# RWKV-6 attention and an exact-GELU MLP on one core: a new order for the first tile, its second tile's loads apart from the weight pieces, and odd chunks of one unit's y in the other partition half

## The chip, the cores and the metric

The kernel runs on one core of one Trainium2 chip. The metric is device time in microseconds (us); lower is better. TensorE is called PE (its weight loads PEld), VectorE DVE, ScalarE ACT, GpSimd POOL, and the queue of SyncE, which issues nearly all transfers, SP.

## The reference

Four sequences of 768 tokens with 8 heads of 48 go through a gated linear recurrence. Its result, as 3072 rows of 384, goes through two matrix products with an exact GELU between them. r, k, v, w, u are float32; the two weight matrices come as float64.

```python
for t in range(S):
    cur = einsum('bhd,bhe->bhde', u[None] * kt, vt)
    y[:, :, t] = einsum('bhd,bhde->bhe', rt, state + cur)
    state = wt[:, :, :, None] * state + einsum('bhd,bhe->bhde', kt, vt)
x = y.transpose(0, 2, 1, 3).reshape(3072, 384)
h = x @ w_in                                   # 384 x 2048
out = (0.5 * h * (1 + erf(h / sqrt(2)))) @ w_out   # 2048 x 384
```

## The kernel before, in words

**Tiles.** There are 8 tiles (NX) of 384 tokens. A tile holds four pairs of heads; the two heads of a pair lie in partitions 0 to 63 and 64 to 127, and the tokens are cut into chunks of 64, six to a tile, even and odd ones taken as pairs. attention(x, unit) computes one tile's y: products of k and r by levels (L485, for tile 1 also L501, for later tiles L653), whose masked parts go to a_sb (DVE L581, ACT L578), decay products on DVE (L552, L563), k transposed on PE (kt_ps L754) and copied to SBUF by ACT (L767), k times v (kv_ps L804), the states chained on DVE (st L836, L831), and y from two sets of products into the same banks: a_sb times v (L857), then the state times r (L900), with small DVE reads (the fences, L867 and L870) between the sets. y is copied to xT, the transposed input of the MLP. Its rows of the fourth pair go through ysb (ACT L926) and three transfers each on SP and ACT (L930).

**The first tile** is the one tile cut into two units: unit 0 holds pairs 0 and 1, unit 1 holds pairs 2 and 3. Each unit has 24 small matmuls for each product. Unit 0's y lies in two single banks, one for even and one for odd chunks (the code calls this split); unit 1's lies in a pair of banks. The small matmuls use one quarter of the PE array each: 64 rows by 64 columns, where the rows are the operands' partition half and the columns are the partition half of the result. In L857 of unit 0 the row half is the chunk's parity p and the column half is the head g. In L900 the row half is the head g and the column half is g too.

**mlp(x)** multiplies a tile by w_in (h_ps L1290 for tiles 0 and 1, L1078 for later ones), applies GELU on ACT (L1293, L1295), and multiplies by w_out (o_ps L1384 for tile 0, L1304 for later ones). Tile 1 and later use sums of weight blocks (t, made on DVE at L946) to save products.

**Weights.** Each matrix comes in 8 pieces of 768 KB (16 in all). A float64 piece goes to a buffer raw (five of them), ACT makes two parts of each number (f L355; e L356 and L358), and DVE shifts and adds them (L367, L371) into w_in_sb or w_out_sb. The first three pieces come in three transfers of 256 KB each, and ahead of each transfer stands a 4-byte DVE write (L229) that holds the transfer back to that point of DVE's order. Tile 1's r, k, w come in eight shares of 288 KB, held back in the same way (L188).

**The order of the work** is written out by hand. Each piece of work is a generator; PLAN holds, for each round x, a string in which one letter takes one step of one stream. What a step issues goes into each engine's own queue in that order, and each queue runs in order. In round 0 the streams are: "." unit 0, "s" unit 1, "f" the beginning of tile 1's attention, "c" weight conversions, "w" the load of tile 1's v, "l" the transfers of the first three weight pieces with tile 1's shares put between them. In round 1 and later "." is mlp(x-1), "s" the rest of tile x's attention, "f" the beginning of the next tile's, "l" the loads of tile x+1, "c" (round 1) the conversions, "w" and "x" sums of weights and of x. After a string, what is left in the streams is issued stream by stream.

Of the kernel before, what the change touches and what calls it, by code (L numbers as in the profile page):

```python
# [21 lines left out]
C = 64  # L22
G = 64
D = 48
T = 384
Q = 2
# [10 lines left out]
NC_SP = 8  # L37
HALFWAY = 2
PLAN = {
    0: ".lls.....sslsc.lsslll.sl.sls.f.sl.lfscsl..sfss.lscfs.lscs.s.ssssclll..s...sss..cs...sw.ccff",  # L40
    1: (
        ".c.scccl..lscssc.cccscxcl..ccc.cscclcccc..ccscs.ccc.cc.ccss.cccccs.c.wcwccssss..c.ccss.ccl"
        ".sswwww.cccccccslwcclllf....sslc...cc...sf.fs.ffff...fffwffwwwwwlc"
    ),
    2: "....s...slw.sswssl.sssss...ss.sss.swsllsslwsww...s...sl..www.wslss..lcs.s.lf.sl..fx.w.xxx....sxxfff.....l",
    3: (
        "wscl..ss..s..sss....s...l.s.ssssssss..s..l.ss...sss..sllssss.ss...s...s...s...sllsssllf.sl"
        ".ff.fxxlx.xx....sffxfff"
    ),
    4: (  # L50
        "......llls..ss.....s....sss..ssss.....llssss..s...ssss...s..lssc..ss.....ssllsss..lfs..lfs"
        ".f..sffx..x.xffxxwfff.xl"
    ),
    5: ".......s...l.lls.s...s..ssssslssss...ss....sss.ssssss...s...ss...l.s..lslllfsss..c.sfffs..l..lwfxxx.xxx.",
    6: (
        "ss.ss....s...s....ss...s...sssls.slss....sss...s...ssss..lss...s..sscw....lll.ssll..sssslf"
        "..sf.f.ffll.x..x.x.ffsffxxx"
    ),
    7: (
        "......s..s...s.s...sss.ss.ss.sss..ss...wwwsss..swssswcs.ss.ww....l.s.wwwsww.wwww..ws.s.ss."  # L60
        "s.wwwwwswwwwww.ww.xxxxxww..xxx.wwsxx.x"
    ),
}

# [12 lines left out]
def kernel(  # L77
# [25 lines left out]
    nc = tc.nc  # L103
# [45 lines left out]
    half = [slice(0, 64), slice(64, 128)]  # L149
# [226 lines left out]
    def attention(x, unit):  # L376

        first = x % HALVES == 0
        parts = range(NPART) if units_of(x) == 1 else range(unit, unit + 1)
# [5 lines left out]
        r, k, w = (bufs[0 if x == 0 or i == 0 and x % 2 == 0 else 1][:, base + i * n_u:base + (i + 1) * n_u]  # L385
                   for i in range(3))
# [6 lines left out]
        xT = xT_of[x]  # L393
# [350 lines left out]
        if x < 2:  # L744
# [49 lines left out]
        def vs(b, i, g):  # L794
            o = ((parts[b] * NI + i) * 2 + g) * D
            return loaded[x][1][:, o:o + G]
# [39 lines left out]
                        nc.vector.tensor_copy(out=stq[:, b * Q:(b + 1) * Q, c], in_=kvs[b][:, :, 0, 0])  # L836


        def swap(b):
            return parts[b] % 2  # L840


        split = x == 0 and parts[0] == 0
        ys = []

        def inside():

            for b in range(np_):
                if split:
                    y = [ps.tile([128, BANK], F32, name="y_ps", tag="mm", bufs=2) for _ in range(2)]  # L850
                else:
                    y_ps = pair("y_ps")
                    y = [y_ps[:, c] for c in range(2)]
                for i in range(NI):
                    for p in range(2):
                        for g in range(2):
                            nc.tensor.matmul(y[p][half[g ^ swap(b)], i * C:(i + 1) * C], lhsT=vs(b, i, g)[half[p]],  # L857
                                             rhs=at[half[p], g, b * NI + i, :], start=(i == 0), stop=True, skip_group_check=True)
                ys.append((y, None if split else y_ps))

# [29 lines left out]
        for i in range(NI):  # L890
            for p in range(2):
                for b in range(np_):
                    q, c3 = divmod(i, N3)
                    for g in range(2):
                        c = 2 * c3 + (p + g) % 2
                        src, c0 = (st, c - 1) if c else (before, NC - 1)
                        if src is None:
                            continue
                        o = ((parts[b] * Q + q) * NC + c0) * D
                        nc.tensor.matmul(ys[b][0][c % 2][half[g ^ swap(b)], i * C:(i + 1) * C],  # L900
                                         lhsT=src[half[g], o:o + G], rhs=rc[half[g], b, i, c % 2],
                                         start=False, stop=True, skip_group_check=True)
        if split:
            for c, copy in enumerate((nc.scalar.copy, nc.vector.tensor_copy)):
                for z in range(2):
                    s = slice(z * G, z * G + D)
                    copy(out=xT[s, 0:Q, :].rearrange("p q (i c t) -> p (q i) c t", c=2, t=C)[:, :, c, :],
                         in_=ys[0][0][c][s, 0:NI * C].rearrange("p (i t) -> p i t", t=C))
            yield
            return  # L910
# [531 lines left out]
    def next_v():  # L1442
        load_v(1, nc.sync)
        yield
# [94 lines left out]
```

## Time and profile before

| what | value |
|---|---|
| median of 3 runs | 586.36 us (585.44 to 586.76) |
| the profiled execution's own time | 586.0 us |
| its span, first to last instruction | 584.1 us |
| PE busy over the span | 570.4 us (98%) |
| DVE, ACT, POOL busy | 460.1 (79%), 286.8 (49%), 8.1 us (1%) |
| granted PE clock | 1.0 |
| first h_ps matmul of tile 0 (L1290) | 44.3 us |
| first o_ps matmul of tile 1 (L1304) | 111.4 us |

In the page's view of 40 slices PE is at nine tenths or more from the fourth slice on; the first three slices, some 44 us, are tile 0's attention. The span from 44 to 111 us is round 1: tile 0's MLP with tile 1's attention. In a timeline row the first number is the start, the second the stretch, then come engine, line, operation and count; in square brackets is the idle time before it and what ended that. "issue" means that the engine waited for nothing that the profile shows. A float32 matmul is recorded as two, each with a weight load of its own.

### The profile page before, as it was taken

To read this page: it belongs to the slowest core of one execution; us is meant where nothing else is said; L and a number is where in the kernel's file an instruction comes from. 1 tells how busy PE (TensorE), PEld (TensorE's weight loads), DVE (VectorE), ACT (ScalarE), POOL (GpSimd) and SP (SyncE) were. 2 spreads that over 40 slices of the span, in tenths; PEclk is the share of its full clock that TensorE was granted. 3 is DMA by queue.
4 is the path that set the end of the run, shared out by engine and by line. 5 is a ranking of instruction groups with operands and counts; after the bars stand their busy time and mean duration, and the time that the engine had idled before them with its cause. 6 is when DMAs were issued, how large, how long until landed. Compare 5 with 4: busy or idle time off the path is not lost.

```text
span 584.1 us, 17192 instructions
## 1 busy us (share of the span) xinstructions
PE 570.4 (98%) x7418; PEld 505.7 (87%) x7418; DVE 460.1 (79%) x820; ACT 286.8 (49%) x672; POOL 8.1 (1%) x21
## 2 busy tenths in 40 slices
PE   7879999999999999999999999999999999999997
PEld 3566566756899999999999999999999999999997
DVE  6879769998879895888859988598859999965532
ACT  2576997332722567336553466345562367423400
POOL 3100000000000000000000000000000000000000
PEclk9999999999999999999999999999999999999999
DMA  7659741220232302341023201440014200210000
GB/s 240 205 158 372 255 171 57 77 80 2 36 103 75 111 2 39 95 122 57 1 55 120 76 21 22 111 140 2 3 34 146 72 3 2 43 39 7 1 15 34
DMA packets 51002, 46.78 MB, mean 80 GB/s; under 512 B 31728, under 2 KB 36080, under 8 KB 50928
## 3 DMA queue, kind: packets, MB, share of 16 engines
q1 hardware_dynamic: 50832, 45.62, 26.0%
q8 instruction: 58, 0.95, 0.7%
q14 instruction: 16, 0.13, 0.1%
q10 hardware_dynamic: 96, 0.07, 0.1%
HBM read 36.24 MB, written 4.72 MB: 70 GB/s over the span
## 4 chain that ended last, share of the span: by engine, by line
PE 93%; DMA 2%; ACT 2%; DVE 1%; issue 1%; SPq 0%; DVEq 0%; ACTq 0%
PE o_ps L1304 35%; PE h_ps L1078 16%; PE u_ps L1078 12%; PE h_ps L1290 11%; PE d L653 4%; PE o_ps L1384 4%; PE kv_ps L804 2%; PE y_ps L857 2%; PE y_ps L900 2%; PE c_ps L1078 2%; PE d L485 2%; DMA rkw<-in_rkw_dram 1%; DMA raw<-in_w_in_dram 1%; PE d L644 0%; ACT a_sb L669 0%
## 5 line engine op out<-in xcount | busy, mean ns | idle before, releaser
L1078 PE MATMUL h_ps<-xT,w_in_sb 128*128 128x192 f32 x408 | 81.5, 331 | 0.0
L1078 PEld LDWEIGHTS h_ps<-xT,w_in_sb 128*128 128x128 f32 x408 | 67.7, 190 | 3.0 <-ACT g L1110 1.1
L1290 PE MATMUL h_ps<-xT,w_in_sb 128*128 128x384 f32 x192 | 64.3, 491 | 0.0
L1290 PEld LDWEIGHTS h_ps<-xT,w_in_sb 128*128 128x128 f32 x192 | 35.7, 190 | 24.6 <-ACT rkw L1295 0.9
L1304 PE MATMUL o_ps<-w_out_sb,g 128*128 128x192 f32 x224 | 39.5, 326 | 0.0
L1304 PEld LDWEIGHTS o_ps<-w_out_sb,g 128*128 128x128 f32 x224 | 37.0, 190 | 0.3
L669 ACT COPY a_sb<-d 32x256 f32<-32x256 f32 (+8 forms) x90 | 32.6, 362 | 4.0 <-PE d L653 2.5
L1304 PE MATMUL o_ps<-w_out_sb,e 128*128 128x192 f32 x176 | 31.3, 329 | 0.0
L1304 PE MATMUL o_ps<-w_out_sb,f 128*128 128x192 f32 x176 | 31.1, 329 | 0.0
L1304 PE MATMUL o_ps<-t,e 128*128 128x192 f32 x176 | 30.9, 328 | 0.0
L1304 PE MATMUL o_ps<-t,s 128*128 128x192 f32 x176 | 30.9, 328 | 0.0
L1304 PE MATMUL o_ps<-t,g 128*128 128x192 f32 x176 | 30.8, 329 | 0.0
L1078 PE MATMUL u_ps<-s,w_in_sb 128*128 128x192 f32 x160 | 29.6, 328 | 0.0
L1304 PEld LDWEIGHTS o_ps<-t,g 128*128 128x128 f32 x176 | 28.7, 190 | 0.3
L1304 PEld LDWEIGHTS o_ps<-w_out_sb,e 128*128 128x128 f32 x176 | 28.7, 190 | 0.3
L1304 PEld LDWEIGHTS o_ps<-t,s 128*128 128x128 f32 x176 | 28.8, 190 | 0.2
L1304 PEld LDWEIGHTS o_ps<-t,e 128*128 128x128 f32 x176 | 28.8, 190 | 0.2
L1304 PEld LDWEIGHTS o_ps<-w_out_sb,f 128*128 128x128 f32 x176 | 28.7, 190 | 0.3
L1293 ACT ACTIVATE g<-h_ps 128x256 f32<-128x256 f32 (+1 forms) x32 | 13.8, 432 | 29.3 <-PE h_ps L1290 29.0
L485 PEld LDWEIGHTS d<-rkw 64*64 64x64 f32 x1056 | 17.3, 135 | 12.5 <-issue 6.9
L653 PE MATMUL d<-kx,rkw 64*64 64x96 f32 x1056 | 27.8, 247 | 0.2 <-ACT a_sb L669 0.2
L686 DVE COPY_PREDICATED a_sb<-quarter,d 128x480 f32<-128x480 uint8 (+5 forms) x54 | 23.1, 438 | 6.3 <-PE d L653 5.0
(247 smaller groups left out, 1188.2 us busy)
## 6 DMA issues: line engine op xcount, KB each, us to landing
rkw<-in_rkw_dram SPq DMA_DIRECT2D x54, 256.0 KB, 3.5
raw<-in_w_out_dram SPq DMA_DIRECT2D x8, 768.0 KB, 4.9
v_in<-in_v_dram SPq DMA_DIRECT2D x8, 584.0 KB, 4.3
raw<-in_w_in_dram SPq DMA_DIRECT2D x5, 768.0 KB, 6.6
out_dram<-o_sb SPq DMA_DIRECT2D x20, 192.0 KB, 2.0
rkw<-kx SPq DMA_DIRECT2D x72, 48.0 KB, 2.0
rkw<-in_rkw_dram SPq DMA_DIRECT2D x6, 384.0 KB, 6.8
raw<-in_w_in_dram SPq DMA_DIRECT2D x9, 256.0 KB, 4.2
```

The source lines that it names most:

```text
L485: nc.tensor.matmul(d[half[p], g, n * width:(n + 1) * width], lhsT=kc[half[g], b, i, p], rhs=right(half[g], b, i, p), start=True, stop=True)
L653: nc.tensor.matmul(o[half[p], i * 3 * C // 2:(i + 1) * 3 * C // 2], lhsT=kc[half[g], n // NI, n % NI, p], rhs=rx[half[g], 2 * n + p], star ...
L669: nc.scalar.copy(out=at[z, g, first:behind, (a + 1) * h:], in_=d[z, :, :, to] if g == slice(None) else d[z, :, to])
L686: nc.vector.copy_predicated(out=an[:, :, :, :, (a + 1) * h:], mask=mask.to_broadcast(data.shape), data=data)
L804: nc.tensor.matmul(kv_ps[half[g], p, i * D:(i + 1) * D], lhsT=k_t(b, i, p, g), rhs=vs(b, i, g)[half[p], 0:D], start=True, stop=True)
L857: nc.tensor.matmul(y[p][half[g ^ swap(b)], i * C:(i + 1) * C], lhsT=vs(b, i, g)[half[p]], rhs=at[half[p], g, b * NI + i, :], start=(i == 0 ...
L900: nc.tensor.matmul(ys[b][0][c % 2][half[g ^ swap(b)], i * C:(i + 1) * C], lhsT=src[half[g], o:o + G], rhs=rc[half[g], b, i, c % 2], start= ...
L1078: nc.tensor.matmul(o, lhsT=lhsT, rhs=rhs, start=start, stop=True, skip_group_check=True)
L1290: nc.tensor.matmul(h_ps, lhsT=w_in_sb[:, f // FI, j, f % FI * 128:(f % FI + 1) * 128], rhs=xT[:, j, :], start=(j == 0), stop=(j == NJ - 1))
L1293: nc.scalar.activation(out=gs[group][:, f % FG, 0:t], in_=h_ps[:, 0:t], func=AF.Gelu)
L1304: nc.tensor.matmul(o, lhsT=lhs(j), rhs=rhs(j), start=start and j == 0, stop=(j == HF - 1), skip_group_check=True)
L1384: nc.tensor.matmul(o, lhsT=block(i, f // HF, f % HF), rhs=w_out_sb[:, f, :], start=(f == 0), stop=(f == NF - 1))
```

## The change

Three things are changed.

1. PLAN's strings for rounds 0 and 1 are written anew. The strings for rounds 2 to 7 get two more turns of all streams at their ends.
2. Tile 1's eight shares, which stood between the weight pieces in stream "l", become a stream of their own, "x".
3. In unit 0 of tile 0, L900 and L857 put the odd chunks' y in the other partition half than the head (swap now returns the chunk's parity c instead of 0), and the copies to xT bring them back (to = z ^ c).

The instructions of the program are the same but for these partition halves and for a few of the wait instructions. On PE, ACT and SP the order differs in rounds 0 and 1 alone; on DVE the weight sums t (L946) come somewhat later and the order is the same again in round 2. The changed file has six more lines ahead of the kernel's code, so that L900 is its L906.

```diff
 PLAN = {
-    0: ".lls.....sslsc.lsslll.sl.sls.f.sl.lfscsl..sfss.lscfs.lscs.s.ssssclll..s...sss..cs...sw.ccff",
+    0: "...sls..l.sxsss.sflcl.sx.ls.l.l.lfsss..sxscxxxsss.x.s..cxss.lsfsssxxfs..s..cl..sscs...wwss.ccls..ffcw",
     1: (
-        ".c.scccl..lscssc.cccscxcl..ccc.cscclcccc..ccscs.ccc.cc.ccss.cccccs.c.wcwccssss..c.ccss.ccl"
-        ".sswwww.cccccccslwcclllf....sslc...cc...sf.fs.ffff...fffwffwwwwwlc"
+        "xc..ccss..cccssc.cccc..sssccc.cccccss.scccccsc.cc.ss.ssswccc.c.ssslcc..scllc...cc.lll.cs.c"
+        "cccclcccllsf.c.xfcccclfl.l.ccc.cc.cffccffff...c.wwsw..w.w...sw.fffxlwwwsswwwww"
     ),
...
-        def swap(b):
-            return parts[b] % 2
+        def swap(b, c):
+            return c if split else parts[b] % 2
...
-                            nc.tensor.matmul(y[p][half[g ^ swap(b)], i * C:(i + 1) * C], lhsT=vs(b, i, g)[half[p]],
+                            nc.tensor.matmul(y[p][half[g ^ swap(b, p)], i * C:(i + 1) * C], lhsT=vs(b, i, g)[half[p]],
...
-                        nc.tensor.matmul(ys[b][0][c % 2][half[g ^ swap(b)], i * C:(i + 1) * C],
+                        nc.tensor.matmul(ys[b][0][c % 2][half[g ^ swap(b, c % 2)], i * C:(i + 1) * C],
...
-                    s = slice(z * G, z * G + D)
-                    copy(out=xT[s, 0:Q, :].rearrange("p q (i c t) -> p (q i) c t", c=2, t=C)[:, :, c, :],
+                    s, to = (slice(a * G, a * G + D) for a in (z, z ^ c))
+                    copy(out=xT[to, 0:Q, :].rearrange("p q (i c t) -> p (q i) c t", c=2, t=C)[:, :, c, :],
...
-                ".": units[0], "s": units[1], "f": following, "c": pieces_of_w, "w": next_v(), "x": iter(()),
-                "l": chain(weight_in(0, True), islice(second, 5), weight_in(1, True), weight_in(2, True), second),
+                ".": units[0], "s": units[1], "f": following, "c": pieces_of_w, "w": next_v(), "x": second,
+                "l": chain(*(weight_in(i, True) for i in range(3))),
```

In queue terms: SP had two parts of the first weight piece, its third, five shares, the six parts of pieces two and three, piece four, then three shares. Now it has two parts, a share, the third part, a part of piece two, a share, two parts of piece two, two of piece three, six shares, the last part of piece three, piece four. In ACT's queue of round 0, where conversions of three pieces stood, two stand; the third comes after unit 0's copies to xT. The eight copies L578 now come ahead of the third of the four pairs L429, L431 (tile 1's scaled r). On PE the last product of unit 0 (24 matmuls of L485) now comes ahead of unit 1's kt_ps instead of behind it. DVE's first L371 moves from ahead of unit 0's last L552 to behind unit 1's state chain.

More of the change, by code (lines that the diff above doesn't have):

```diff
@@ L39 @@
 PLAN = {
-    0: ".lls.....sslsc.lsslll.sl.sls.f.sl.lfscsl..sfss.lscfs.lscs.s.ssssclll..s...sss..cs...sw.ccff",
+    0: "...sls..l.sxsss.sflcl.sx.ls.l.l.lfsss..sxscxxxsss.x.s..cxss.lsfsssxxfs..s..cl..sscs...wwss.ccls..ffcw",
     1: (
-        ".c.scccl..lscssc.cccscxcl..ccc.cscclcccc..ccscs.ccc.cc.ccss.cccccs.c.wcwccssss..c.ccss.ccl"
-        ".sswwww.cccccccslwcclllf....sslc...cc...sf.fs.ffff...fffwffwwwwwlc"
-    ),
-    2: "....s...slw.sswssl.sssss...ss.sss.swsllsslwsww...s...sl..www.wslss..lcs.s.lf.sl..fx.w.xxx....sxxfff.....l",
+        "xc..ccss..cccssc.cccc..sssccc.cccccss.scccccsc.cc.ss.ssswccc.c.ssslcc..scllc...cc.lll.cs.c"
+        "cccclcccllsf.c.xfcccclfl.l.ccc.cc.cffccffff...c.wwsw..w.w...sw.fffxlwwwsswwwww"
+    ),
+    2: (
+        "....s...slw.sswssl.sssss...ss.sss.swsllsslwsww...s...sl..www.wslss..lcs.s.lf.sl..fx.w.xxx."
+        "...sxxfff.....l.slxwc.slxwc"
+    ),
     3: (
         "wscl..ss..s..sss....s...l.s.ssssssss..s..l.ss...sss..sllssss.ss...s...s...s...sllsssllf.sl"
-        ".ff.fxxlx.xx....sffxfff"
+        ".ff.fxxlx.xx....sffxfff.slxwc.slxwc"
     ),
@@ L51 @@
         "......llls..ss.....s....sss..ssss.....llssss..s...ssss...s..lssc..ss.....ssllsss..lfs..lfs"
-        ".f..sffx..x.xffxxwfff.xl"
+        ".f..sffx..x.xffxxwfff.xl.slxwc.slxwc"
     ),
-    5: ".......s...l.lls.s...s..ssssslssss...ss....sss.ssssss...s...ss...l.s..lslllfsss..c.sfffs..l..lwfxxx.xxx.",
+    5: (
+        ".......s...l.lls.s...s..ssssslssss...ss....sss.ssssss...s...ss...l.s..lslllfsss..c.sfffs.."
+        "l..lwfxxx.xxx..slxwc.slxwc"
+    ),
     6: (
         "ss.ss....s...s....ss...s...sssls.slss....sss...s...ssss..lss...s..sscw....lll.ssll..sssslf"
-        "..sf.f.ffll.x..x.x.ffsffxxx"
+        "..sf.f.ffll.x..x.x.ffsffxxx.slxwc.slxwc"
     ),
@@ L60 @@
         "......s..s...s.s...sss.ss.ss.sss..ss...wwwsss..swssswcs.ss.ww....l.s.wwwsww.wwww..ws.s.ss."
-        "s.wwwwwswwwwww.ww.xxxxxww..xxx.wwsxx.x"
+        "s.wwwwwswwwwww.ww.xxxxxww..xxx.wwsxx.x.slxwc.slxwc"
     ),
```

## The prediction

> **What bounds the kernel now.** I read the share of each engine first, then the busy time by stage, then the chain that ended last, then ACT's and PE's timelines where that chain leaves PE. By stage (from, to, length, then busy time of PE, PEld, DVE, ACT, POOL, each with its count):
>
> ```profile
> 9.76:44.25 34.49, 27.89 (x1072) 21.33 (x1073) 28.46 (x76) 19.16 (x37) 2.89 (x5) 1.00 0.56 183
> 44.25:111.40 67.15, 67.15 (x943) 42.76 (x941) 56.54 (x81) 50.92 (x85) 0.00 (x0) 1.00 0.56 197
> ```
>
> The change reorders these two stages. In the second PE is never idle, and PE has the same matmuls there after the change, so a new order can gain next to nothing there and can only lose. In the first PE is idle for 6.6 us. The chain shows who holds it (start, us, what):
>
> ```profile
> 21.80 4.33 DMA raw<-in_w_in_dram
> 26.23 0.93 ACT f L355
> 27.16 0.92 ACT e L356
> ...
> 33.70 0.95 PE kv_ps L804 x48
> 34.65 0.81 PE kt_ps L754 x6
> 35.45 0.86 PE y_ps L857 x48
> 36.99 1.24 issue
> 38.89 1.84 DVE st L831 x10
> 40.91 1.32 PE y_ps L900 x36
> 42.34 1.98 PE d L501 x94
> ```
>
> Tile 0's y waits for kv_ps, and kv_ps for ACT, which is late because a weight piece landed late. ACT's timeline of that stretch:
>
> ```profile
> 26.23 0.93 ACT L355 ACTIVATE f<-raw 128x768 f32<-128x768 f32 x1 [3.95 <-DMA raw<-in_w_in_dram]
> 27.07 1.01 ACT L356 ACTIVATE e<-raw,two 128x768 f32<-128x768 uint32 x1
> 28.10 1.08 ACT L358 ACTIVATE e<-raw 128x768 f16<-128x768 f32 x1
> 30.58 2.57 ACT L578 COPY a_sb<-d 16x192 f32<-16x192 f32 x8
> 33.17 0.86 ACT L767 COPY g<-kt_ps 128x384 f32<-128x384 f32 x2
> 35.16 0.86 ACT L767 COPY g<-kt_ps 128x384 f32<-128x384 f32 x2 [0.30 <-PE kt_ps L754]
> ```
>
> ACT stood 3.95 us for the second piece, converted it, scaled two pairs of r (29.05 to 30.67) and then made the eight copies L578, so that kt_ps, done at about 31.7, was copied only from 33.17. The second thing that holds PE is the line "issue". PE's timeline between two such gaps:
>
> ```profile
> 19.50 0.45 PE L485 MATMUL d<-rkw 64*64 64x64 f32 x11 [0.85 <-issue]
> 20.41 0.93 PE L485 MATMUL d<-rkw 64*64 64x64 f32 x48
> 21.80 0.93 PE L485 MATMUL d<-rkw 64*64 64x64 f32 x48
> 23.20 0.46 PE L485 MATMUL d<-rkw 64*64 64x64 f32 x15
> 24.59 0.73 PE L485 MATMUL d<-rkw 64*64 64x64 f32 x33 [0.94 <-issue]
> ```
>
> With three pairs of warming matmuls between them, 11+48+48+15+6 = 128 matmuls and as many weight loads lie between the gaps: 256 instructions. The third gap (36.99, 1.24 us) comes three times 256 later. The instruction queue moves 58 packets, 0.95 MB, so 16 KB a packet. So PE runs out of instructions where a block of 256 ends before the next is there. In the trace's transfer records the packet for the third gap started 36.02, 2.07 us after PE had entered the block before (33.95), took 0.93, and PE went on 1.27 after its end, at 38.22. The next block's packet started 1.40 after that, took 0.92, and PE entered that block at 41.95.
>
> The Trainium skill, "Runtime: NRT & Kernel Launch", section "Instruction fetch mechanics", gives blocks of 16 KiB or 256 instructions and calls the crossing "mostly hidden". The size agrees with the trace; the hiding does not, where 64x64 matmuls run at some 18 ns a record: three gaps of 0.85 to 1.24 us.
>
> **The change, part by part.**
>
> *ACT up to kv_ps.* On SP the second piece's last part has two of tile 1's shares ahead of it where it had five. Alone, such a part landed 2.77 us after its issue (27.34 to 30.10); behind the shares it took 4.33. Issued about 21, it lands between 23.8 and 25.3 instead of 26.13, and its conversion (2.95) ends between 26.8 and 28.3. The copies L578 then follow their products (the second left PE at 27.77 + 0.93 = 28.7) and end near 28.7 + 4 x 0.32 = 30.0; the third pair of r (0.87) ends by 30.9. kt_ps still waits for DVE (L552, at 30.87), whose list up to there is the same work; unit 0's last product ahead of it fits in PE's idle time (0.77 and 0.87 us of waits there). From kt_ps to its first copy takes 0.58 (34.58 to 35.16), one copy 0.49, and 0.04 to PE. So kv_ps starts at 30.87 + 0.58 + 0.53 = 31.98, not 33.70: **-1.72**. Bounds: 0 if ACT is still late by as much; -2.2 if DVE's path also gains the 0.5 by which ACT is then early.
>
> *From kv_ps to the second kv_ps.* The fourth pair of r (0.87) now stands ahead of the second pair of L767. Counted from the first kv_ps, L767 ends at 0.45, two L778 at 1.40, the pair at 2.26, the L767 at 3.24, and kv_ps ends at 3.73. Before, with its gap, it ended at 38.57 - 33.70 = 4.87. So the pair hides under the instruction gap if that stays as long: **0**. Without the gap it would end 3.29 in the old order: the pair costs 0.44 once that cover is gone.
>
> *The instruction gap itself* moves with PE's own entry into the block: 0 if its packet again starts 2.07 after. Between the shortest and the longest start seen in this stage (1.1 and 2.73) it is -0.97, cut by the 3.73 above to some -1.1 at most, or +0.66. I take 0, since shares and a part stand just ahead of it again (now also a 768 KB piece, issued near 31). The two gaps at 18.6 and 23.7 fall after the same 256 instructions; DVE lost 1.40 us behind the second. Taken 0; -1.0 (gone) to +0.7 (a packet as late as the latest).
>
> *The partition halves.* Unit 0's L900 used two quarters of the array: 40 records in 1.32 us. Tile 1's L900, on four, shows 96 in 1.56, 16 ns each: 40 would take 0.65, so -0.67. But a block ends at the 35th of these 40 records (5 of kv_ps, 40 and 48 of y, and 35 are 128). PE enters it at best 1.40 + 0.92 + 1.25 = 3.57 after the last entry; before it took 41.95 - 38.22 = 3.73. So only **-0.17** shows, and up to -0.67 if the earlier gap is shorter. The copies to the other half are taken at the price of L907 (0.55); no row shows a copy across halves, bounds -0.1 and +0.5 (the cover is the L501 matmuls, 1.98 us, and the xT copies wait 0.45).
>
> A rule speaks against this part: the Trainium skill, "TensorEngine Tiling (Array Packing)", section "Restrictions and Gotchas", says that different row tiles cannot access the same PSUM bank at once. Now both rows write both of unit 0's banks, in different partitions. By it the -0.67 would go, and the total would be smaller by the 0.17; no row of before shows that mix held at once.
>
> *Round 1.* PE is full before; the sum of its matmuls is the same, and small matmuls follow large ones as often (eight times). The third conversion now comes first in round 1 on ACT, and the transfers of w_out follow later. ACT has 14 conversions of 3.02 there where it had 13: 50.9 + 3.0 of 67 us. DVE's L371 (0.95) moved behind the state chain, where DVE stood 1.15 for kv_ps. **0**, bounds -0.5 (PEld's few waits) and +2.0 (one conversion and a half late). From the first o_ps of tile 1 on, PE's order is the same; three DVE sums t come later, and are first read 40 us on (at 156).
>
> *SP, POOL.* Tile 1's last share is issued near 30 instead of at 33.02, ahead of its use in L501 (42.3, then 40.4); POOL's list is the same. 0.
>
> Sum: -1.72 - 0.17 = -1.89. The profiled execution took 586.0, so 584.1; the median lies 0.36 above it: **584.5**.
>
> **The rivals.** No change is what lies within 0.2%, 1.2 us, of 586.36.
>
> *The forecast* (gap unchanged, round 1 full): 583.8 to 585.1. Chance 0.58. For it: the late piece and the copies L578 stand on the chain by themselves.
>
> *More*: the gap at 18.6 or 23.7 goes too, because one share, not a part and shares, stands ahead of the packet: another -0.7 to -1.4, 583.4. Against it: DVE is 82 to 90% busy there. Chance 0.08.
>
> *The supply of instructions sets the end of the stage*: PE enters the block 1.7 earlier, but its packet waits behind shares and the 768 KB piece issued at 30 to 31, to about 35 to 35.5; PE resumes 2.2 later at some 37.5, 0.7 before the old 38.22. With the 0.17 that leaves 0.9: 585.5. For it: packets started late (2.07 to 2.73) just behind shares. Against it: packets in round 1 did not wait for 768 KB pieces (0.8 at 51.84). Chance 0.20.
>
> *Slower*: the last five w_out conversions (15.1 us on ACT) come after the last GELU near 81, and DVE puts 3.5 us of L414 between them, while o_ps takes a new piece each 2.6 us from 83 on. By the rows the tightest piece is ready about 0.9 ahead of its matmul; every us that ACT, DVE or a landing is late beyond that stops a PE that is otherwise full. It decides from 0.9 + 1.9 = 2.8 late; at 4 late it is 587.6. For it: four pieces bunched at 46 to 58 landed 9 to 11 us after issue. Against it: ACT was busy only 0.85 of 10 us at 100 to 110. Chance 0.14.
>
> *That the halves do nothing* would cost the 0.17: 584.6, within the forecast.
>
> Faster: 0.58 + 0.08 = 0.66; same 0.20; slower 0.14. The range runs from the middle of "more", 583.2, to the edge of "no change" and a little beyond, 586.5.
>
> **What would show it.** Right: kv_ps first near 32.0, ACT's wait for the second piece under 1.5 us, L501 near 40.1, h_ps first at 42.4, the first o_ps of L1304 (after: L1310) near 109.5, PE full between. The L900 of unit 0 at 16 ns a record, with an "issue" gap in its last five. Wrong: an "issue" gap over 1.3 us before the second kv_ps (supply), or o_ps waiting for DVE's L371 between 85 and 105 (slower).

## The result

The changed kernel is slower. Its median is 587.88 us over 19 runs (585.42 to 589.28), and the kernel before, run beside it, has 585.75 us over 19 runs (584.61 to 587.83). The ratio is 1.0027, with a 95% interval of 1.0016 to 1.0037. I had forecast 584.5 us.

The profiled execution of the changed kernel is one of its shortest (585.75 us, span 583.6): its first d product starts at 8.08 us, as its first transfers landed early, and at 9.76 in the profiled execution before. From that mark on it is the longer one, so I compare stages and distances. First the two stages, in windows from tile 0's first d product to its first h_ps and from there to tile 1's first o_ps, then the two 3.41 us stretches at the gap (from, to, length, then the busy time of PE, PEld, DVE, ACT and POOL, each with its count, then granted clock, DMA share and GB/s):

```profile
8.08:42.72 34.64, 27.50 (x1062) 22.47 (x1073) 28.71 (x77) 17.30 (x35) 2.88 (x5) 0.95 0.62 195
42.72:111.21 68.49, 67.12 (x943) 43.02 (x940) 56.43 (x78) 53.53 (x88) 0.00 (x0) 1.00 0.55 193
32.99:36.40 3.41, 1.13 (x56) 1.01 (x53) 1.62 (x7) 0.14 (x1) 0.00 (x0) 1.00 0.31 120
36.41:39.82 3.41, 3.18 (x86) 2.99 (x82) 2.28 (x14) 0.48 (x1) 0.00 (x0) 0.50 0.02 5
```

Round 0 is no shorter than before (34.64 us against 34.49), although ACT has stopped being late. Round 1 is 1.34 us longer with the same busy PE time (67.12 against 67.15), so PE stood idle there. And for 3.41 us PE had half its clock, which the profiled execution before had nowhere in these stages. ACT's timeline shows the late piece gone: a wait of 1.30 us for the second piece instead of 3.95, and the copies L584 (L578 before) ahead of the pair of r.

```profile
23.27 0.92 ACT L361 ACTIVATE f<-raw 128x768 f32<-128x768 f32 x1 [1.30 <-DMA raw<-in_w_in_dram]
26.07 2.55 ACT L584 COPY a_sb<-d 16x192 f32<-16x192 f32 x8
29.63 0.86 ACT L773 COPY g<-kt_ps 128x384 f32<-128x384 f32 x2
```

PE's timeline shows what became of it:

```profile
30.16 0.95 PE L810 MATMUL kv_ps<-v_in,g 64*64 64x48 f32 x48 [0.24 <-ACT g L773]
31.04 0.88 PE L760 MATMUL kt_ps<-ident,rkw 128*128 128x128 f32 x6
31.85 0.93 PE L863 MATMUL y_ps<-a_sb,v_in 64*64 64x64 f32 x48
32.80 0.93 PE L810 MATMUL kv_ps<-v_in,g 64*64 64x48 f32 x42
36.00 0.32 PE L810 MATMUL kv_ps<-v_in,g 64*64 64x48 f32 x6 [2.28 <-issue]
...
38.05 1.54 PE L863 MATMUL y_ps<-a_sb,v_in 64*64 64x64 f32 x44
39.89 0.80 PE L906 MATMUL y_ps<-rkw,st 64*64 64x64 f32 x35 [0.30 <-DVE fence L873]
```

kv_ps starts 30.16 - 8.08 = 22.08 us after the first d product, against 33.70 - 9.76 = 23.94 before: 1.86 us earlier. Then the instruction gap ahead of the last six products of the second kv_ps (the last five before) is 2.28 us where it was 1.24. Behind it, 44 products of y take 1.54 us at half clock, where 43 of them took 0.86. The rows before:

```profile
38.23 0.26 PE L804 MATMUL kv_ps<-v_in,g 64*64 64x48 f32 x3 [1.24 <-issue]
39.56 0.86 PE L857 MATMUL y_ps<-a_sb,v_in 64*64 64x64 f32 x43
```

In round 1 there is a gap that the kernel before did not have, inside tile 1's d product:

```profile
73.07 1.35 PE L491 MATMUL d<-rkw 64*64 64x32 f32 x74
75.79 0.55 PE L491 MATMUL d<-rkw 64*64 64x32 f32 x22 [1.37 <-issue]
76.27 4.14 PE L1296 MATMUL h_ps<-xT,w_in_sb 128*128 128x384 f32 x12
```

The trace's transfer records for the instruction queue say why. Of each block of 256 PE instructions: when PE entered the block before it, how much later the packet started, when it had landed, and when PE went on.

```
                           entered  packet starts  landed   PE goes on
block at the second kv_ps
  before                    33.95      + 2.07      36.95      38.22
  changed                   30.49      + 3.11      34.54      36.00
block inside tile 1's d (round 1)
  changed                   70.19      + 3.27      74.36      75.79
```

In the kernel before, the packet of round 0 started as the last bytes of three shares came in (issued 32.11 to 33.02, landed by 36.47); piece four had landed by 34.16. In the changed kernel its neighbours are the last part of piece three (issued 28.98), the 768 KB piece four (29.36, first bytes landed 33.57) and a share. In round 1 five of tile 2's transfers and two pieces of w_out were issued from 65.77 to 70.39, around PE's entry. A full DMA alone did not hold a packet up that long: in round 1 before, with a DMA share of 1.05 and 402 GB/s from 50 to 60, one started 0.8 us after entry, at 52.64. Why that one did not wait is not shown.

PE goes through that block of round 1 in 4.2 us, since two d products (96 matmuls each) have only 6 of h_ps between them; as the packet took 0.9 and PE went on 1.4 after it had landed, it would have had to start within some 1.9 us of entry to hide (my estimate: 4.2 - 0.9 - 1.4).

My theory from here on, "S": the gain on ACT is real, but the supply of instructions takes it back, as the packet waits behind transfers in both rounds; and the longer idle time of PE now and then costs it half its clock for 3.41 us. Rivals: the partition halves do it; round 1's late conversions do it; the gaps are a fixed price of these block ends.

### The profile page after: what moved, and what is told of

The parts are those of the page before. It is cut to its first block, busy times and chain, and to the rows that moved or that the text cites. A ratio compares the mean times of both kernels' runs of the same rounds, so it can differ in the third digit from the quotient of the medians.

```text
span 583.6 us, 17180 instructions
## 1 busy us (share of the span) xinstructions
PE 568.8 (97%) x7407; PEld 506.6 (87%) x7418; DVE 459.7 (79%) x820; ACT 287.6 (49%) x672; POOL 8.0 (1%) x21
## 4 chain that ended last, share of the span: by engine, by line
PE 91%; DVE 3%; DMA 2%; issue 2%; ACT 1%; SPq 0%; ACTq 0%; DVEq 0%
PE o_ps L1310 33%; PE h_ps L1084 16%; PE u_ps L1084 12%; PE h_ps L1296 11%; PE d L659 4%; PE o_ps L1390 4%; PE kv_ps L810 2%; PE d L491 2%; PE y_ps L863 2%; PE y_ps L906 2%; PE c_ps L1084 2%; DMA rkw<-in_rkw_dram 2%; DMA raw<-in_w_in_dram 1%; DVE kx L420 1%; PE d L650 0%
```

## The experiments

Over all runs, the distances between marks in the profiled executions are these, in us. "Round 0" is from tile 0's first d product to its first h_ps, "round 1" from there to tile 1's first o_ps. The marks are compared as distances, since the first d product itself starts between 8.1 and 9.8 us, as its first transfers land. A profiled execution is one run of several: those of e1 and e4 are the slowest of theirs, that of e12 is within 0.01 us of its fastest.

| kernel | round 0 | gap at second kv_ps | round 1 | gap in tile 1's d | at half clock | ratio to before, 95% interval |
|---|---|---|---|---|---|---|
| before | 34.49 | 1.24 | 67.15 | none | none | |
| changed | 34.64 | 2.28 | 68.49 | 1.37 | 3.41, round 0 | 1.0027 [1.0016, 1.0037] |
| e1 | 37.79 | 2.63 | 68.46 | 1.36 | 6.83, round 0 | 1.0042 [1.0024, 1.0060] |
| e2 | 34.41 | 1.41 | 67.27 | none | none | 1.0003 [0.9994, 1.0013] |
| e3 | 33.58 | 2.21 | 67.12 | none | none | 0.9993 [0.9979, 1.0007] |
| e4 | 34.92 | 1.62 | 72.43 | 1.77 | 6.83, round 1 | 1.0047 [1.0030, 1.0065] |
| e5 | 32.45 | 0.35 | 70.26 | 1.04 | 3.41, round 1 | 1.0037 [1.0021, 1.0053] |
| e7 | 33.77 | 2.08 | 68.00 | 0.90 | none | 1.0016 [1.0000, 1.0033] |
| e9 | 33.36 | 0.71 | 68.03 | none | none | 0.9988 [0.9976, 1.0000] |
| e10 | 35.55 | none | 67.03 | none | 3.41, round 0 | 1.0012 [0.9996, 1.0028] |
| e11 | 32.78 | 0.71 | 67.09 | none | none | 0.9987 [0.9974, 1.0000] |
| e12 | 32.36 | 0.35 | 67.73 | 0.62 | none | 0.9998 [0.9988, 1.0008] |
| e13 | 34.78 | 1.24 | 67.23 | none | none | 0.9999 [0.9989, 1.0010] |
| e14 | 32.36 | none | 68.53 | 1.43 | none | 1.0000 [0.9984, 1.0016] |

The kernels before beside them had medians of 584.81 (e1 to e4), 584.84 (e5 to e10) and 585.16 us (e11 to e14).

**e1: the changed kernel without the partition halves.**

```diff
-            return c if split else parts[b] % 2
+            return parts[b] % 2
...
-                    s, to = (slice(a * G, a * G + D) for a in (z, z ^ c))
+                    s, to = (slice(a * G, a * G + D) for a in (z, z))
```

> The changed kernel with its new strings and stream, but with unit 0's odd chunks of y back in the head's own partition half. Theory S (supply of instructions and the clock): the gap marked issue before the second kv_ps stays at 1.9 to 2.6 us and a window of half clock follows it, since neither has to do with the halves; unit 0's L906 is slower by 0.1 to 0.7; the kernel is 0.2 to 0.5% slower than before. Theory H (both row halves now write both banks, and that slows the y products of unit 0): the slow stretch of L863 and L906 at 36 to 40 us goes, they run at 16 to 33 ns a record there, and the time is at or under that of before.

It measured 587.47 us, ratio 1.0042, with nine of its eleven runs below full clock. So the halves are not what makes the change slow. PE's timeline of e1 has the gap again, longer than in the changed kernel, and here two windows at half clock:

```profile
38.73 0.46 PE L810 MATMUL kv_ps<-v_in,g 64*64 64x48 f32 x6 [2.63 <-issue]
...
41.09 1.53 PE L863 MATMUL y_ps<-a_sb,v_in 64*64 64x64 f32 x44
42.93 2.08 PE L906 MATMUL y_ps<-rkw,st 64*64 64x64 f32 x38 [0.31 <-DVE fence L873]
```

**e2: the kernel before with the halves alone.**

```diff
-        def swap(b):
-            return parts[b] % 2
+        def swap(b, c):
+            return c if split else parts[b] % 2
...
-                    s = slice(z * G, z * G + D)
+                    s, to = (slice(a * G, a * G + D) for a in (z, z ^ c))
```

> The kernel before, with the old strings and the old stream, and only the partition halves of unit 0's odd chunks changed. Theory S: the gap before the second kv_ps is 1.0 to 1.5 us as before; unit 0's L906 takes 0.65 to 0.8 us for 40 records instead of 1.32, and 0 to 0.5 us of that shows: ratio 0.999 to 1.000. Theory H: L863 and L906 of unit 0 take over 35 ns a record and the kernel is 0.1 to 0.3% slower than before.

It measured 584.75 us, ratio 1.0003: nothing to be seen. PE's timeline tells why: 35 records of L900 take 0.85 us where 37 took 1.32 (S had 0.65 to 0.8 for 40), and then PE stands at the block end as forecast.

```profile
40.02 0.85 PE L900 MATMUL y_ps<-rkw,st 64*64 64x64 f32 x35 [0.50 <-DVE fence L867]
41.05 0.28 PE L900 MATMUL y_ps<-rkw,st 64*64 64x64 f32 x3 [0.19 <-issue]
```

From the first L900 to the long row of L501 it is 41.20 - 40.02 = 1.18 us, against 42.14 - 40.91 = 1.23 before.

**e3: the new plan of round 0 with the old plans of the later rounds.** PLAN[1] to PLAN[7] are the old strings, all else is as changed.

```diff
-        "xc..ccss..cccssc.cccc..sssccc.cccccss.scccccsc.cc.ss.ssswccc.c.ssslcc..scllc...cc.lll.cs.c"
-        "cccclcccllsf.c.xfcccclfl.l.ccc.cc.cffccffff...c.wwsw..w.w...sw.fffxlwwwsswwwww"
+        ".c.scccl..lscssc.cccscxcl..ccc.cscclcccc..ccscs.ccc.cc.ccss.cccccs.c.wcwccssss..c.ccss.ccl"
+        ".sswwww.cccccccslwcclllf....sslc...cc...sf.fs.ffff...fffwffwwwwwlc"
```

> The changed kernel with the old string for round 1 and for rounds 2 to 7, so that only round 0's order, tile 1's stream and the halves are new. Theory S: round 0 has the long gap (1.9 to 2.6 us) and a window of half clock, and first h_ps comes at the old distance from the first product (34.2 to 34.9 us); round 1 has no gap over 0.5 us and takes 67.0 to 67.5 us from h_ps to the first o_ps of tile 1; ratio 0.999 to 1.002. Theory R (round 1's order alone is at fault, and round 0 kept its forecast gain): ratio 0.996 to 0.998.

It measured 584.10 us, ratio 0.9993. Round 1 is whole again (67.12 us), and the gap in round 0 is still 2.21 us:

```profile
36.92 0.33 PE L789 MATMUL kv_ps<-v_in,g 64*64 64x48 f32 x6 [2.21 <-issue]
```

The packet of that block started 3.25 us after entry. The profiled execution lost no clock there, and round 0 took 33.58 us, 0.6 less than S had given at least.

**e4: the kernel before with the halves and the new plan of round 1.** PLAN[0], PLAN[2] to PLAN[7] and the streams "l" and "x" of round 0 are the old ones, PLAN[1] is the new one (the diff of e3, the other way round). The partition halves of e2, which changed no time there, are in it too.

> The kernel before with the halves and with the new string for round 1 alone; round 0's string and stream are the old ones. Theory S: the gap in d (L491, old L485) of tile 1 near 75 us is there, 1.0 to 2.0 us, since its packet of instructions stands behind tile 2's loads and the w_out pieces that this string issues between 65 and 73 us, and round 1 takes 68.2 to 69 us from h_ps to the first o_ps of tile 1; ratio 1.001 to 1.003. Rival: the gap came from what round 0 left for round 1 (a conversion more); then round 1 has no gap and the ratio is 0.999 to 1.000.

It measured 587.29 us, ratio 1.0047. The new order of round 1 is slow without the new order of round 0. PE's timeline and the stretches around that place:

```profile
77.51 0.85 PE L470 MATMUL d<-rkw 64*64 64x32 f32 x21 [1.77 <-issue]
```

```profile
73.79:77.20 3.41, 1.94 (x78) 1.29 (x77) 2.20 (x6) 2.65 (x7) 0.00 (x0) 1.00 1.05 407
77.21:84.03 6.82, 6.52 (x30) 3.91 (x30) 4.32 (x5) 3.02 (x5) 0.00 (x0) 0.50 0.09 34
43.64:116.07 72.43, 70.48 (x944) 44.70 (x941) 56.38 (x78) 51.27 (x85) 0.00 (x0) 0.95 0.53 183
```

PE stood 1.77 us with the DMA engines full (share 1.05, 407 GB/s), and then ran 6.83 us at half clock. 72.43 - 1.77 - 6.83 / 2 = 67.25, the old length: gap and clock are all of it in this execution. The packet had started 3.59 us after entry.

**e5: the changed kernel with piece four held back** until DVE has finished a conversion. It goes out in three parts of 256 KB, each behind a 4-byte DVE write; so it does in all the runs below that move it.

```diff
-        for _ in weight_in(i + 3):
+        for _ in weight_in(i + 3, i == 0):
```

> The changed kernel with one thing undone: the fourth piece of w_in (768 KB, one transfer issued at 29.36 us) is held back, in three transfers that go out only after VectorE has finished the conversion at 33.64 us. Theory S (the packet with the next 256 TensorE instructions waits behind transfers, and the longer idle time drops TensorE's clock): the packet for the block that begins at the last six products of the second kv_ps starts at most 2.3 us after TensorE enters the block before it (3.11 in the changed kernel), the gap there is 1.0 to 1.5 us instead of 2.28, most runs lose no half-clock window in round 0, the distance from the first d product to the first h_ps of tile 0 is 31.9 to 33.3 us instead of 34.64, round 1 keeps its gap (68.0 to 68.8), and the time falls by 1.0 to 2.7 us against the changed kernel, to 585.2 to 586.9 (ratio to before 1.000 to 1.0035). Rival (the gap is a fixed cost of this block end, whatever is in flight, or the time was lost elsewhere): gap 2.1 to 2.4 us, distance 34.3 to 35, ratio 1.003 as the changed kernel.

The packet started 1.23 us after entry, the gap fell to 0.35 us, and round 0 took 32.45 us, 2.19 less. That is S's direction, and further than S had it (a gap of 1.0 to 1.5); it speaks against a fixed price of the block end. The time was 587.46 us all the same, ratio 1.0037, outside what S had given. Two things show in PE's timeline:

```profile
34.67 0.33 PE L810 MATMUL kv_ps<-v_in,g 64*64 64x48 f32 x6 [0.35 <-issue]
41.12 0.88 PE L1296 MATMUL h_ps<-xT,w_in_sb 128*128 128x384 f32 x2 [0.68 <-DMA xT<-ysb]
42.18 2.20 PE L1296 MATMUL h_ps<-xT,w_in_sb 128*128 128x384 f32 x6 [0.17 <-DMA xT<-ysb]
74.26 0.55 PE L491 MATMUL d<-rkw 64*64 64x32 f32 x22 [1.04 <-issue]
```

The piece, now at 35.2 to 36.1, runs into the small transfers that bring y to xT, and h_ps waits for those. Round 1 has its gap, and a half-clock window behind it. By the profiled execution these give back only part of the gain; the median of seven runs, four of which lost clock, says all of it. Another 1.0 us of this execution lies far behind, between the kv_ps of tiles 6 and 7 (65.95 us, and 64.96 in e14), where the programs are the same; the cause is not shown.

**e7: the changed kernel with three of tile 2's transfers of round 1 later.**

```diff
-        "xc..ccss..cccssc.cccc..sssccc.cccccss.scccccsc.cc.ss.ssswccc.c.ssslcc..scllc...cc.lll.cs.c"
-        "cccclcccllsf.c.xfcccclfl.l.ccc.cc.cffccffff...c.wwsw..w.w...sw.fffxlwwwsswwwww"
+        "xc..ccss..cccssc.cccc..sssccc.cccccss.scccccsc.cc.ss.ssswccc.c.ssslcc..scllc...cc..cs.c"
+        "ccccllllcccllsf.c.xfcccclfl.l.ccc.cc.cffccffff...c.wwsw..w.w...sw.fffxlwwwsswwwww"
```

> The changed kernel with one thing moved in round 1: the three transfers of tile 2 that SyncE issues at 69.46 to 70.39 us are issued after the next three h_ps steps instead (the first of them from about 80 us on). Theory S: the packet of the block that ends in tile 1's d product starts 1 to 2 us after TensorE enters the block before it instead of 3.27, the gap of 1.37 us there is gone or below 0.4, the distance from the first h_ps of tile 0 to the first o_ps of tile 1 is 67.0 to 67.4 instead of 68.49, the half-clock window that some runs lose at that place is gone, and the time falls by 1.2 to 2.2 us against the changed kernel, to a ratio to before of 0.999 to 1.0015. Rival L (round 1 is longer for its late conversions of w_out, not for the gap): the distance stays at 68.2 to 68.8 though the gap is gone, and the ratio stays near 1.003. Rival for the sign: tile 2's later loads become a wait of their own in round 1 or 2, and the time is no shorter.

The packet started 2.67 us after entry instead of 3.27, the gap fell from 1.37 to 0.90 us, and round 1 to 68.00. That is the right direction and a third of the size expected: the three transfers moved only to 72.46, and a piece of w_out issued at 68.78 (landed 73.58) still stood ahead of the packet. The ratio of 1.0016 lies some 0.6 us below the changed kernel's, about the 0.5 us that the profiled execution shows, and half of the least that S had given. Round 0 still has its gap, and ten of the twelve runs lost clock.

**e9: e3 with piece four held back as in e5.**

> The new plan for round 0 with the old plan for round 1 (the run e3, 0.9993 of before), and the fourth piece of w_in held back as in e5. Theory S: gap at the second kv_ps 1.0 to 1.5 us instead of 2.21, first d product to first h_ps 32.3 to 33.0 us instead of 33.58, round 1 as before (67.1), granted clock 1.0 in most runs, and 582.3 to 583.5 us beside a before of 584.8, ratio 0.996 to 0.998: faster than both kernels. Rival (gap and clock have nothing to do with the transfers): ratio 0.999 as e3, gap 2.2.

Ratio 0.9988. The packet started 1.42 us after entry, the gap is 0.71 us instead of 2.21, and all twelve runs kept the full clock, where six of e3's eleven had not. The time did not fall clearly with it (e3 had 0.9993), since h_ps waits for the transfers of y, twice:

```profile
42.88 0.89 PE L1275 MATMUL h_ps<-xT,w_in_sb 128*128 128x384 f32 x2 [0.49 <-DMA xT<-ysb]
44.49 1.88 PE L1275 MATMUL h_ps<-xT,w_in_sb 128*128 128x384 f32 x5 [0.72 <-DMA xT<-ysb]
```

**e10: e9 with ten warm-up matmuls instead of sixteen.**

```diff
-    keep_warm(16)
+    keep_warm(10)
```

> As e9, and ten warm-up matmuls instead of sixteen at the start: twelve TensorE instructions fewer, so that the block end falls just behind the last product of the second kv_ps instead of six products ahead of it. Theory S: the gap stays at 1.0 to 1.5 us but lies behind kv_ps, VectorE's 2.1 us of state work runs beside it, and the first h_ps comes 0.4 to 0.9 us earlier than in e9, 31.6 to 32.5 us behind the first d product; ratio to before 0.995 to 0.9975. Rival (the gap belongs to these products and their operands, not to a count of instructions): the gap stays ahead of the last six products of kv_ps, and the time is that of e9. Rival on the other side: fewer warm-up matmuls leave TensorE slower at the start, or the block ends of later stages fall worse, and it is 0.5 us or more slower than e9.

The block end moved out of kv_ps as meant, but the rival on the other side held: 585.28 us, ratio 1.0012. TensorE stood 2.96 us before the first d product, and that product ran at half clock:

```profile
3.54 2.46 PE L232 MATMUL warm<-zeros 128*128 128x512 bf16 x7
8.97 1.56 PE L470 MATMUL d<-rkw 64*64 64x64 f32 x48 [2.96 <-DMA rkw<-in_rkw_dram]
10.27 1.53 PE L470 MATMUL d<-kx,rkw 64*64 64x64 f32 x48
12.05 0.38 PE L232 MATMUL warm<-zeros 128*128 128x512 bf16 x1 [0.25 <-issue]
12.36 0.93 PE L470 MATMUL d<-rkw 64*64 64x64 f32 x48
```

The same 48 matmuls take 1.56 us here and 0.93 at full clock. Eight of its twelve runs lost clock. But this is not all of the 2.19 us by which its round 0 is longer than e9's: h_ps waited 2.26 us for the transfers of y, where e9's first wait was 0.49.

```profile
44.52 5.72 PE L1275 MATMUL h_ps<-xT,w_in_sb 128*128 128x384 f32 x17 [2.26 <-DMA xT<-ysb]
```

So the price of fewer warm-up matmuls is not measured apart from that wait.

**e11: e3 with piece four between the two dangers.** Its three parts go out behind the packet's request and well ahead of the transfers of y.

```diff
-    0: '...sls..l.sxsss.sflcl.sx.ls.l.l.lfsss..sxscxxxsss.x.s..cxss.lsfsssxxfs..s..cl..sscs...wwss.ccls..ffcw',
+    0: '...sls..l.sxsss.sflcl.sx.ls.l.l.lfsss..sxscxxxsss.x.s..cxss.lsfsssxxfs..s..c.lll.sscs...wwss.ccls..ffcw',
...
-        for _ in weight_in(i + 3):
+        for _ in weight_in(i + 3) if i else ():
...
-                "l": chain(*(weight_in(i, True) for i in range(3))),
+                "l": chain(*(weight_in(i, True) for i in range(4))),
```

> As e9 (new plan for round 0, old plan for round 1), but the fourth piece of w_in goes out between the two dangers: its three transfers are released ahead of VectorE's first state copy (about 32.5 us), behind the request for the packet of the block end, and 6 us ahead of the small transfers of y. Theory S: the packet starts at most 2.0 us after TensorE enters the block before it (3.25 in e3, 1.42 in e9), gap 0.4 to 1.3 us, no wait of h_ps for the transfers of y (e9 lost 0.49 and 0.72 us there), first d product to first h_ps 32.2 to 33.0 us, granted clock 1.0 in nearly all runs, ratio to before 0.996 to 0.9985. Rival (what e9 won at the gap is lost again wherever the 768 KB are put, since they take 2.3 us of the transfers' time): h_ps or the conversions wait for it, distance 33.3 to 34, ratio 0.9985 to 1.0005 as e3 and e9.

It measured 583.99 us beside 585.16, ratio 0.9987. The packet started 1.33 us after entry, the gap is 0.71 us, h_ps waits for nothing, and the two stages together take 99.87 us against 101.64 before:

```profile
8.99:41.77 32.78, 26.48 (x1063) 21.24 (x1073) 28.80 (x80) 17.55 (x36) 2.86 (x5) 1.00 0.63 199
41.77:108.86 67.09, 67.07 (x943) 42.72 (x940) 56.42 (x81) 52.99 (x88) 0.00 (x0) 1.00 0.57 198
```

This is the lowest ratio of the study (e9 has 0.9988), clearly below the changed kernel's; against the kernel before the interval just reaches 1.0. Nine of its twelve runs had the full clock, with a median of 583.18 us; the three others 586.33.

**e14: the changed kernel, whole, with piece four as in e11.**

> The changed kernel, whole, with the fourth piece of w_in put where e11 has it and nothing else. Theory S: round 0 mended as in e11 (gap 0.4 to 1.3 us, first d product to first h_ps 32.2 to 33.2 us instead of 34.64), round 1 as in the changed kernel: its gap of about 1.4 us and now and then a half-clock window, 68.3 to 70.3 us; ratio to before 1.000 to 1.003, about 0.001 below the changed kernel's 1.0027. Rival (round 0 was not where the loss lay): ratio as the changed kernel, 1.0025 to 1.004.

Ratio 1.0000 instead of 1.0027 (the intervals touch at 1.0016), with one transfer moved, in three parts, and nothing else. The packet started 0.95 us after entry, and the gap is gone: PE stands less than 0.1 us inside the second kv_ps, which is now one row (a gap of 0.69 us shows at the next block end instead, in unit 0's L906), and round 0 takes 32.36 us, 2.28 less than in the changed kernel. Round 1 keeps its gap of 1.43 us:

```profile
32.88 1.33 PE L810 MATMUL kv_ps<-v_in,g 64*64 64x48 f32 x48
```

```profile
8.33:40.69 32.36, 26.21 (x1064) 21.08 (x1073) 28.53 (x80) 17.50 (x36) 2.85 (x5) 1.00 0.67 219
40.69:109.22 68.53, 67.10 (x944) 43.11 (x941) 56.37 (x78) 53.33 (x88) 0.00 (x0) 1.00 0.54 189
```

**e12: e14 with five of tile 2's transfers later.**

```diff
-        "xc..ccss..cccssc.cccc..sssccc.cccccss.scccccsc.cc.ss.ssswccc.c.ssslcc..scllc...cc.lll.cs.c"
-        "cccclcccllsf.c.xfcccclfl.l.ccc.cc.cffccffff...c.wwsw..w.w...sw.fffxlwwwsswwwww"
+        "xc..ccss..cccssc.cccc..sssccc.cccccss.scccccsc.cc.ss.ssswccc.c.ssslcc..scc...cc..cs.c"
+        "ccccllllllcccllsf.c.xfcccclfl.l.ccc.cc.cffccffff...c.wwsw..w.w...sw.fffxlwwwsswwwww"
```

> As e14, and five of tile 2's transfers in round 1 issued only after the block end inside tile 1's d product (three of them in e7). Theory S: both gaps mended: the packet for the block end in round 1 starts at most 2.0 us after TensorE enters the block before it (3.27 in the changed kernel, 2.67 in e7), the gap there is below 0.4 us, first h_ps of tile 0 to first o_ps of tile 1 is 66.9 to 67.6 us, first d product to first h_ps 32.2 to 33.2, granted clock 1.0 in most runs, and the ratio is 0.996 to 0.999. Rival (round 1 is longer for its late conversions, not for its gap): 68.0 us or more without a gap, ratio 0.9995 to 1.002.

Ratio 0.9998. The gap in round 1 is down to 0.62 us (packet 2.33 after entry, still behind pieces of w_out) and the round to 67.73 us. S had the direction, but asked for less than 0.4 us, at most 67.6 and a ratio of 0.999 at most. The two stages together take 100.09 us, 1.55 less than before. The medians differ by 0.65 us and the interval holds 1.0, so a gain over the kernel before is not shown.

**e13: the kernel before with piece four later.**

```diff
-    0: ".lls.....sslsc.lsslll.sl.sls.f.sl.lfscsl..sfss.lscfs.lscs.s.ssssclll..s...sss..cs...sw.ccff",
+    0: ".lls.....sslsc.lsslll.sl.sls.f.sl.lfscsl..sfss.lscfs.lscs.s.ssssclll..s...xxxsss..cs...sw.ccff",
...
-        for _ in weight_in(i + 3):
+        for _ in weight_in(i + 3) if i else ():
...
-                ".": units[0], "s": units[1], "f": following, "c": pieces_of_w, "w": next_v(), "x": iter(()),
+                ".": units[0], "s": units[1], "f": following, "c": pieces_of_w, "w": next_v(), "x": weight_in(3, True),
```

> The kernel before, with its fourth piece of w_in (issued at 29.04 us) put ahead of the first state copy in the same way, about 34.7 us. Theory S: the last shares of unit 1 (32.1 to 33.4 us) no longer stand behind the piece, the packet of the block end at the second kv_ps starts 1.0 to 1.6 us after TensorE enters the block before it instead of 2.07, the gap falls from 1.24 to 0.3 to 0.9 us, first d product to first h_ps is 33.6 to 34.2 us instead of 34.49, ratio 0.998 to 1.0. Rival: the shares come no earlier and the piece, later, collides with the small transfers of y: 34.5 or more, ratio 1.000 to 1.002.

Nothing changed: gap 1.24 us, packet 1.90 us after entry, ratio 0.9999. Here S as I had put it was wrong. In the old order PE enters that block so late (33.95) that piece four has all but landed (34.16). By the transfer records the three shares were under way just ahead of the packet there: in both kernels the last of them comes in from 36.0 on, and the packet starts then (36.02, and 35.98 in e13). The piece hurts only in the new order, in which PE comes 1.86 us earlier.

## Why the prediction was wrong

*ACT up to kv_ps, -1.72.* Right: -1.86, with the wait for the second piece at 1.30 us ("under 1.5"). The later marks that I had named (L501 near 40.1, h_ps at 42.4) look nearly met, at 40.5 and 42.72, but only because this execution's first product starts 1.68 us earlier; counted from there they are not.

*From kv_ps to the second kv_ps, 0.* Right in effect: it is 3.57 us from the first product of kv_ps to the gap, 0.28 more than before, and PE would have waited there in any case, since the packet came later still.

*"The instruction gap itself ... I take 0".* This step failed. I took the packet to start 2.07 us after PE's entry again and gave +0.66 as the upper bound; it started 3.11 after, beyond the latest that I had seen (2.73), and the gap grew by 1.04 us. That is also the sign that I had named for being wrong (a gap over 1.3 us). I had let the packet's start move with PE's entry; in these traces it did not, but came when the transfers ahead of it were through or nearly so. From the first d product, the gap ended at 38.23 - 9.76 = 28.47 us before and at 36.00 - 8.08 = 27.92 in the changed kernel: of 1.86 us gained, 0.55 was left. That is my rival "the supply of instructions sets the end of the stage" (0.7), to which I had given 0.20. e5, e9, e11 and e14, where the packet started 0.95 to 1.42 us after entry, show that it was piece four's place in the queue that held it up. e14's round 0, 32.36 us, is 2.13 shorter than before, where the forecast had 1.89 for it: the sum is near for a packet that is not held up, in part by luck, as kv_ps came 2.04 earlier there and the gap that I had kept is gone, with 0.69 us lost at the next block end and 0.86 instead of 0.49 at the fence.

*The clock* was in no step. In the changed kernel 16 of 19 runs had a mean granted clock under 0.9985, with a median of 588.17 us; the three others 586.02, near the 585.75 before. Of the 94 runs of the kernel before beside the experiments, 21 were under it. So, by these few runs, the longer gaps took the gain away and the clock made most of the loss. A window of 3.41 us at half clock costs up to 1.7 us, and all of that where PE is the limit, as in e4. With piece four out of the way the share of such runs fell to 5 of 12 in e14, and with round 1's gap at 0.62 us too to 2 of 11 in e12.

*The partition halves, -0.17.* Right in kind: the records run faster, 24 ns each (35 in 0.85 us) against 36 before, though not at the 16 that I took from tile 1, and the block end takes it: 0.05 of the 0.17 shows in e2's trace. The rule of the Trainium skill, "TensorEngine Tiling (Array Packing)", section "Restrictions and Gotchas", by which two row tiles cannot access the same PSUM bank at once, did not keep them at 36 ns, though the rows now write both banks, in different partitions. Whether it is what keeps them from 16 is not shown.

*"Round 1 ... 0".* This step failed too: it measured +1.34, inside the bounds of -0.5 and +2.0, and neither bound's reason was the cause. I looked at conversions and at o_ps. The supply of instructions I had as a rival for round 0 alone, and held the packets of the old round 1 against it, where a block lasts 5.9 us or more and hides them. The new order puts two d products with only 6 h_ps products between them, so that a block lasts 4.2 us, and seven transfers of 256 to 768 KB around its packet. Round 1 less its gap and half of its half-clock time is 67.12 us in the changed kernel, 67.10 in e7, 67.10 in e14, 67.11 in e12, 67.25 in e4 and 67.5 in e5, and 67.15 before. So the rival "slower" had the sign, and not the reason: PE waited for no conversion.

Together, in the profiled execution: -1.86 to kv_ps, +0.28 from there to the gap, +1.04 at the gap, +0.70 from there to h_ps, where the half clock falls, and +1.34 in round 1.

What stays open: counting only runs at full clock (a mean of 0.9985 or more), of the kernel before too, most medians agree with the stages: e3 is 0.95 us shorter than before (0.94 by its stages), e9 0.25 (0.25), e14 0.66 (0.75), e11 1.73 (1.77). But e12 is 0.56 us shorter where its stages say 1.55, and e5, with three such runs, 1.55 longer, where its stages without the half clock are 0.6 shorter. Where in a run the clock is lost I see only in the profiled ones.

## What to carry to other kernels

A shorter chain helps only if the instructions are there when it gets there. In this kernel small matmuls used up a block of 256 in some 4 us, so look in the transfer records at what stands ahead of each packet, at the time at which PE would enter after the change. Moving one 768 KB transfer back by 2 to 4 us, in three parts, was worth 0.27% here (1.0027 to 1.0000), nearly as much as I had forecast for the whole change (1.89 of 586 us, 0.32%). When an order is written anew, look at what each block of instructions is made of (here matmuls of 18 ns or of 330), not only at sums.

## What the runs showed that I had not expected

The half-clock windows lie on a grid of 3.413 us: in e1 they begin at 37.81 and 587.35 us, 161.0 such steps apart, in e4 at 77.21 and 589.21 (150.0), in e10 at 8.54 and 585.39 (169.0); the later of each is the idle end of the program. Here are the grid windows around two drops, the last of which follows an idle time of 1.04 us alone; first e1, then e5:

```profile
34.39:37.80 3.41, 1.71 (x92) 1.48 (x90) 2.57 (x12) 0.75 (x2) 0.00 (x0) 1.00 0.52 190
37.81:44.64 6.83, 5.60 (x126) 5.41 (x128) 3.34 (x15) 0.48 (x1) 0.00 (x0) 0.50 0.09 22
```

```profile
71.84:75.25 3.41, 2.37 (x99) 2.05 (x99) 2.03 (x5) 3.21 (x8) 0.00 (x0) 1.00 0.99 381
75.26:78.67 3.41, 3.41 (x7) 1.81 (x6) 3.27 (x4) 2.11 (x3) 0.00 (x0) 0.50 0.05 17
```

The windows before a drop had PE busy for 26% (e10), 33% (changed), 50% (e1), 57% (e4) and 70% (e5) of their time. But windows with 45% (e7), 46% (e10, 42.67 to 46.09) and 58% (e14) were followed by full clock, so the busy share alone does not decide it, and what does is open. The grid starts at another moment in each run, which may be why a gap of the same size (2.28 us in the changed kernel, 2.21 in e3) costs clock in one run and none in another. The Trainium skill, "TensorE: Matmul & The Clock Gate", Part 1, tells of a free-running activity window of some 3.4 us with half rate after an idle one, and warns of idle gaps over 3.4 us. The grid agrees; the limit does not, as gaps of 1.04 to 2.96 us were followed by half clock here.
